# The first batch of an mLSTM and FNet kernel, moved to half chunks

## The chip, the cores and the metric

The kernel runs on one core of a Trainium2 chip. Its time is the device time of one execution in microseconds (us); several executions are timed and the median is given. The core has five instruction streams that run beside each other and wait for one another through semaphores: PE (TensorE, matrix products, with its weight loads), DVE (VectorE), ACT (ScalarE), POOL (GpSimd), and SP (SyncE, which here only issues transfers between memories). Each stream works strictly in the order written into it.

## The reference, cut to what matters

Two blocks are chained. The first is a gated recurrence over 768 tokens, for 4 batches of 8 heads with 40 features each:

```python
for t in range(S):
    m_new = np.maximum(f_gate[:, :, t] + m, i_gate[:, :, t])
    f_stab = np.exp(f_gate[:, :, t] + m - m_new)
    i_stab = np.exp(i_gate[:, :, t] - m_new)
    m = m_new
    C = f_stab[..., None, None] * C + i_stab[..., None, None] * np.einsum('bhd,bhe->bhde', vt, kt)
    n = f_stab[..., None] * n + i_stab[..., None] * kt
    h_tilde = np.einsum('bhde,bhe->bhd', C, qt)
    denom = np.maximum(np.abs(np.einsum('bhd,bhd->bh', n, qt)[..., None]), 1.0)
    y[:, :, t] = sigmoid(o_gate[:, :, t]) * h_tilde / denom
```

The second takes the heads side by side as 320 features per token and does

```python
u = x + real(fft(fft(x, axis=1), axis=2))       # over tokens, then over features
un = (u - mean(u)) / sqrt(var(u) + 1e-6)        # per token
out = u + relu(un @ w_ch1) @ w_ch2              # 320 -> 1280 -> 320
```

The two weight matrices arrive as 64-bit floats and are turned into 32-bit ones on the chip, piece by piece.

## The kernel before, in words

Tokens are worked on in 6 chunks of 128 per batch. The recurrence becomes, in each chunk, scores of keys against queries weighted by exponentials of running maxima, plus the queries times the state of all earlier chunks. The 768x768 transform uses symmetries: chunks are paired as (0,5), (1,4), (2,3), and three of them (`BACKWARDS` = 0, 1, 3) hold their tokens in reverse order, so that sums and differences of a pair ("folds", `mix_fold`) go straight into the products (`mix_seq`, `mix_tail`). Then come the products over features (`mix_feat`), the sum with x and its mean and variance (`mix_add`), centring and transposing (`mix_center`, `mix_turn`, `mix_turn_out`), and the two layers (`mlp_in` and so on).

The order of all work is written out by hand: `at(slot, phase, function, arguments)` puts a step into a plan, and the plan is emitted in order of slot and phase, into each engine's list. The slots run over the whole kernel: the recurrence of batch 0 lies in slots 0 to 21, its transform in 16 to 30, its layers from slot 31; the recurrence of batch 1 lies beside the layers of batch 0, and so on. Before the plan, `gates()` computes cumulative sums and running maxima of the gates for all batches at once, on 32 rows (batch and head) by 768 tokens.

Batches 1 to 3 use the *half-chunk form* (`plan_halves`, functions `halves_...`): chunks are split in two halves of 64 tokens; maxima and decays are read back from DRAM copies (`M_d`, `G_d`) spread over rows; results come out with tokens on partitions; for a backward chunk, `halves_rows` moves the result to its place in x by two or three transfers. The products of one chunk are issued in the order: queries times state, half of the within-chunk products, scores of the next chunk, new state of the next chunk, the other half.

Batch 0 uses the *whole-chunk form* (`plan_mlstm`, functions `mlstm_...`): maxima are spread over 128 rows by products with a unit column (`spread_max`, L221), weights have 128 keys by 128 queries per head (`mlstm_exp` L491, `mlstm_weigh` L545), results come out with features on partitions (`mlstm_from_state` L553, `mlstm_from_chunk` L560), are copied by ACT (`mlstm_gather`, L583 to L601), transposed by PE (`mlstm_turn`, L611), and finished by DVE (`mlstm_finish`, L712 to L720) directly into x. What batches 1 to 3 need in half-chunk form is made late from batch 0's arrays (`halves_of_chunks`, L329 to L362; `other_halves`; `maxima_out`).

SP's list holds all transfers: inputs `qk` (two transfers a chunk), `kvt`, `so`; the pieces of the weights (`raw`, 0.66 MB each, loaded by `Piece.load`, then `take` on DVE, `convert` on ACT, `join` on DVE); the tables of the transform (`load_tables`: `ds_sb` 1.18 MB, `dd_sb` 0.66 MB); `Gb` (decays spread from `G_d`). Eight completion semaphores are used in turn, so a transfer is issued only when the one eight places earlier has landed.

Of the kernel before, what the change touches and what calls it, by code (L numbers as in the profile page):

```python
# [10 lines left out]
FP = mybir.dt.float32  # L11
BF = mybir.dt.bfloat16
# [3 lines left out]
OP = mybir.AluOpType  # L16
# [37 lines left out]
def kernel(  # L54
# [28 lines left out]
    ps_early = ExitStack()  # L83
    ps_s, ps_h = (ps_early.enter_context(tc.tile_pool(name=n, bufs=2, space=PSUM)) for n in ("ps_s", "ps_h"))

    turn = iter("3210321032120312031230123012012301023130201320132013203120123021320321")
# [17 lines left out]
    h_first = const.tile([L, NP, 1], FP, name="h_first")  # L104
# [6 lines left out]
    C_bufs = [const.tile([L, NP, L], FP, name=f"C{n}") for n in range(3)]  # L111
    states = [t.rearrange("p n t -> p (n t)")[:, i * 2 * L:(i + 1) * 2 * L] for t in C_bufs for i in range(2)]
# [3 lines left out]
    Cd_bufs = [s_last[:, n * NP * D1:(n + 1) * NP * D1].rearrange("p (n m) -> p n m", m=D1) for n in range(2)]  # L116
    hT_bufs = [const.tile([L, NP, L], FP, name=f"h{n}") for n in range(2)]
# [18 lines left out]
    def idle_products(n, first=False):  # L136
        pw = bank("pi", [L, 2 * L]) if first else ps_s.tile([L, 2 * L], FP, name="pi", tag="ps")
        for i in range(n):
            nc.tensor.matmul(pw, rest[:, 0:L], rest, start=True, stop=True, skip_group_check=True)


    def gates(gp):
        f_sb = gp.tile([BH, NT, L], FP, name="f_sb")
        free = w2_sb.rearrange("p f m -> p (f m)")
        M, a = (free[0:n, (i + 1) * S:(i + 2) * S].rearrange("p (c t) -> p c t", t=L) for i, n in enumerate((L, BH)))
        nc.sync.dma_start(out=f_sb.rearrange("p c t -> p (c t)"), in_=f_gate.rearrange("b h s -> (b h) s"))
        nc.sync.dma_start(out=a.rearrange("p c t -> p (c t)"), in_=i_gate.rearrange("b h s -> (b h) s"))
        keep = gp.tile([BH, NT, L], FP, name="keep")
        shift = gp.tile([BH, NT, L], FP, name="shift")
        m_in = gp.tile([BH, NT, 1], FP, name="m_in")  # L150
        F = gp.tile([BH, NT, L], FP, name="F")
        g, wk = (x_bufs[1].rearrange("p c m -> p (c m)")[0:n, i * S:(i + 1) * S].rearrange("p (c t) -> p c t", t=L)
                 for i, n in enumerate((L, BH)))
        nM = gp.tile([BH, NT], FP, name="nM")
        M3 = gp.tile([3 * BH, NT, L], BF, name="M3")
        below = gp.tile([BH, NT, L], BF, name="below")
        sel = gp.tile([3 * BH, BH], BF, name="sel")
        ident_b, later_b = (gp.tile([L, L], BF, name=n) for n in ("ident_b", "later_b"))
# [7 lines left out]
        nc.gpsimd.memset(later_b, 0.0)  # L166
        nc.gpsimd.affine_select(out=later_b, in_=later_b, compare_op=OP.is_ge, fill=-M_INIT, base=0, pattern=[[1, L]],
                                channel_multiplier=-1)
        nc.scalar.copy(out=ident_b, in_=ident)
        for i in range(3):  # L170
            nc.scalar.copy(out=sel[i * BH:(i + 1) * BH], in_=ident[0:BH, 0:BH])
# [3 lines left out]
        nc.vector.memset(M[:, 0:2], 0.0)  # L175
        for t in C_bufs:
            nc.scalar.copy(out=t.rearrange("p (two n) t -> p two (n t)", two=2),
                           in_=rest.unsqueeze(1).to_broadcast([L, 2, 2 * L]))
# [7 lines left out]
        w1_pieces[1].load()  # L186
        for t in hT_bufs + Cd_bufs + [h_first]:
            nc.gpsimd.memset(t, 0.0)

        def flat(t, s):  # L190
            return t[0:BH, s].rearrange("p c t -> p (c t)")
# [5 lines left out]
        def maxima(s, initial):  # L197
            c0, c1 = s.start, s.stop
# [5 lines left out]
            nc.vector.tensor_scalar(out=nM[:, s], in0=M[0:BH, s, L - 1], scalar1=-1.0, scalar2=None, op0=OP.mult)  # L204
# [1287 lines left out]
```

## Time and profile before

| | us |
|---|---|
| median of 3 executions | 391.76 (391.52 to 393.21) |
| the profiled execution, its own time | 392.19 |
| span of its instructions | 390.4 |
| PE busy in the span | 379.6 (97%) |
| DVE busy | 278.0 (71%) |
| ACT busy | 172.1 (44%) |
| POOL busy | 134.9 (35%) |
| mean granted clock of PE | 0.999 |

The profiled execution's own time is 1.8 us more than its span and 0.4 us above the median. A line of a timeline reads: start, length, engine, line of the kernel, operation, output<-input, shape, count; in brackets the idle time before it and what ended it. A line of the stage table reads: stretch, its length, busy time of PE, PEld (weight loads), DVE, ACT and POOL with counts of instructions, PE's granted clock, the share of the 16 DMA engines that was busy, and GB/s.

### The profile page before, as it was taken

How to read it: one execution, taken by the hardware profiler on the slowest of the kernel's cores; microseconds unless marked ns; L12 is line 12 of the kernel's file. 1: busy time of each engine (PE TensorE's matmuls, PEld its weight loads, DVE VectorE, ACT ScalarE, POOL GpSimd, SP SyncE). 2: the span in 40 equal slices, each digit the busy share in tenths (PEclk: the TensorE clock that was granted, in tenths of full speed). 3: DMA queues.
4: the chain of work that ended last, by engine and by line, in shares of the span. 5: the costliest groups of instructions: out<-in, count | busy, mean ns of one | idle time of the engine just before them, and what ended most of it. 6: DMA issues, size and time to landing. Idle time of an engine off the chain costs nothing.

```text
span 390.4 us, 10585 instructions
## 1 busy us (share of the span) xinstructions
PE 379.6 (97%) x4174; PEld 277.3 (71%) x4174; DVE 278.0 (71%) x671; ACT 172.1 (44%) x481; POOL 134.9 (35%) x237
## 2 busy tenths in 40 slices
PE   8999899999999999999999999999999999999996
PEld 6777555656667777765569998755588996556996
DVE  7789988499599587476975699777655785346652
ACT  6887357477543233655462314554530133545000
POOL 5739504467954442173254134541500000020000
PEclk9999999999999999999999999999999999999999
DMA  7887499579394345437700626400000000000101
GB/s 224 287 235 204 159 254 255 179 214 271 109 231 116 122 116 150 149 102 184 182 2 28 174 80 192 135 20 2 0 2 34 6 30 34 2 0 0 35 34 35
DMA packets 25631, 44.78 MB, mean 115 GB/s; under 512 B 5727, under 2 KB 14766, under 8 KB 25454
## 3 DMA queue, kind: packets, MB, share of 16 engines
q1 hardware_dynamic: 25582, 44.11, 38.9%
q8 instruction: 33, 0.54, 0.6%
q14 instruction: 16, 0.13, 0.1%
HBM read 38.49 MB, written 4.12 MB: 109 GB/s over the span
## 4 chain that ended last, share of the span: by engine, by line
PE 78%; DVE 14%; issue 3%; ACT 3%; POOL 1%; DVEq 0%; ACTq 0%; POOLq 0%
PE po L1240 20%; PE pm L1121 15%; PE po L1184 8%; PE pm L1059 7%; PE ph L519 4%; PE pm L1126 4%; PE pu L938 4%; PE ps L519 3%; PE pm L1050 2%; PE put L981 2%; PE pz L907 1%; PE pz L895 1%; DVE h L1130 1%; DVE so L716 1%; PE pM L221 1%
## 5 line engine op out<-in xcount | busy, mean ns | idle before, releaser
L1190 DVE SCALAR_TENSOR_TENSOR x<-po,rstd,x 128x160 f32<-128x160 f32 (+1 forms) x69 | 27.1, 394 | 37.4 <-PE po L1240 32.5
L1130 DVE TENSOR_TENSOR h<-h,pm 128x384 f32<-128x384 f32 x60 | 30.5, 548 | 27.1 <-PE pm L1121 12.6
L652 POOL TENSOR_TENSOR C<-C,decB 128x164 f32<-128x164 f32 x30 | 15.9, 531 | 67.5 <-DVE C L667 56.1
L1121 PE MATMUL pm<-uT,w_sb 128*128 128x384 f32 x90 | 37.7, 506 | 1.3 <-DVE uT L1109 0.6
L491 ACT ACTIVATE W<-W,colT 128x64 f32<-128x64 f32 x144 | 37.5, 339 | 0.4 <-DMA W<-M_d 0.4
L1184 PE MATMUL po<-w_sb,h 128*128 128x320 f32 x120 | 34.3, 435 | 0.0
L515 POOL TENSOR_SCALAR_AFFINE_SELECT W<-W 64x512 f32<-64x512 f32 x36 | 27.3, 759 | 10.6 <-ACT W L491 9.1
L1005 POOL TENSOR_TENSOR t<-rstd 128x6 f32<-128x6 f32 x12 | 3.3, 273 | 79.9 <-DVE v L999 79.4
L1059 PE MATMUL pm<-uT,w_sb 128*128 128x384 f32 x80 | 29.2, 500 | 0.1
L1184 PEld LDWEIGHTS po<-w_sb,h 128*128 128x128 f32 x120 | 22.3, 190 | 9.5 <-issue 0.6
L1240 PE MATMUL po<-T,S 128*128 128x160 f32 x180 | 27.8, 301 | 0.3 <-DVE x L1190 0.3
L501 POOL TENSOR_TENSOR qg<-qk,Gb 128x512 f32<-128x512 f32 (+1 forms) x21 | 27.1, 1290 | 1.7 <-DMA qk<-in_qkT 1.6
L1240 PEld LDWEIGHTS po<-T,S 128*128 128x128 f32 x180 | 25.5, 190 | 1.7 <-DVE x L1190 0.5
L1121 PEld LDWEIGHTS pm<-uT,w_sb 128*128 128x128 f32 x90 | 15.5, 189 | 15.6 <-DVE h L1130 6.7
L1240 PE MATMUL po<-w_sb,h 128*128 128x160 f32 x180 | 26.3, 300 | 0.0
L1240 PEld LDWEIGHTS po<-w_sb,h 128*128 128x128 f32 x180 | 25.2, 190 | 1.4 <-DVE x L1190 0.3
L986 ACT COPY uT<-put 128x384 f32<-128x384 f32 x24 | 11.2, 477 | 30.1 <-PE put L981 30.1
L507 POOL TENSOR_TENSOR vw<-kvt,colT 128x328 f32<-128x328 f32 x23 | 19.7, 859 | 13.1 <-DMA qk<-in_qkT 10.1
L1177 ACT ACTIVATE h<-h 128x384 f32<-128x384 f32 x45 | 23.1, 520 | 2.0 <-DVE h L1130 2.0
L1126 PE MATMUL pm<-uT,w1t_sb 64*128 64x384 f32 x120 | 23.4, 508 | 0.0
L1059 PEld LDWEIGHTS pm<-uT,w_sb 128*128 128x128 f32 x80 | 14.1, 189 | 9.6 <-issue 1.9
L974 ACT ACTIVATE uc<-x 128x384 f32<-128x384 f32 x24 | 14.4, 613 | 12.6 <-DVE x L966 11.1
(241 smaller groups left out, 843.4 us busy)
## 6 DMA issues: line engine op xcount, KB each, us to landing
kvt<-in_kv SPq DMA_DIRECT2D x24, 336.0 KB
qk<-in_qkT SPq DMA_DIRECT2D x48, 160.0 KB
raw<-in_w SPq DMA_DIRECT2D x10, 640.0 KB
Gb<-G_d SPq DMA_DIRECT2D x36, 128.0 KB
W<-M_d SPq DMA_DIRECT2D x36, 128.0 KB
so<-in_o SPq DMA_DIRECT2D x24, 160.0 KB
out<-x SPq DMA_DIRECT2D x24, 160.0 KB
x<-so SPq DMA_DIRECT2D x9, 140.0 KB
```

Source lines behind the costliest of these rows:

```text
L491: nc.scalar.activation(out=k.W[:, h, :], in_=M, func=AF.Exp, scale=-1.0, bias=colT[:, c, 0, b * H + h:b * H + h + 1])
L501: nc.gpsimd.tensor_tensor(out=k.qg[:, :, t], in0=k.qk[:, 0, :, t], in1=k.Gb[:, :, t], op=OP.mult)
L515: nc.gpsimd.affine_select(out=W, in_=W, compare_op=OP.is_ge, fill=0.0, base=base, pattern=[[0, H], [step, LH]], channel_multiplier=-1)
L519: nc.tensor.matmul(out, w, x, start=start, stop=True, skip_group_check=True)
L1059: nc.tensor.matmul(k.pm[i], w1_sb[:, ch, f0:f0 + L], u[2 * ch], start=(ch == 0 and not ahead), stop=(ch == 1 and ahead), skip_group_check= ...
L1121: nc.tensor.matmul(bank, w, u, start=start, stop=True, skip_group_check=True)
L1126: nc.tensor.matmul(bank, block(w1t_sb, i)[rows], mlp_u(gr, 1)[rows], start=False, stop=True, skip_group_check=True)
L1130: nc.vector.tensor_tensor(out=h, in0=h, in1=bank, op=OP.add)
L1177: nc.scalar.activation(out=h, in_=h, func=AF.Relu, scale=-1.0)
L1184: nc.tensor.matmul(k.po[gr, i], hidden(gr, f)[:, i * L:(i + 1) * L], w2_sb[:, f, :], start=(f == 0), stop=(f == NFF - 1))
L1190: nc.vector.scalar_tensor_tensor(out=u, in0=po, scalar=k.rstd[:, c:c + 1], in1=u, op0=OP.mult, op1=OP.add)
L1240: nc.tensor.matmul(po, a[:, f], w[:, f], start=start and f == 0, stop=f == half - 1, skip_group_check=True)
```

## The change

Batch 0 takes the half-chunk form as well; `plan_mlstm` and its functions go, and `plan_first` orders the halves functions for batch 0. Its parts:

- `gates()` works out maxima, decays and key weights for halves from the start, for all batches; `halves_of_chunks` and `other_halves` go. The keys' terms are the biases of the exponentials. The maxima of a chunk are spread by 16 products over 64 columns instead of 8 over 128, into one bank instead of two. Key weights of chunks 2 to 5 are exponentiated in one ACT instruction (`weights_of_others`), and so prepared by one DVE instruction; the same is done for the decays (`decays_of_others`).
- Results come out with tokens on partitions: no transposes, no whole-chunk copies; ACT copies one chunk's result out of the accumulators (`halves_heads`) and DVE finishes from that copy. Chunks 0, 1 and 3 of batch 0 get to x by transfers (`halves_rows`), and chunk 2 passes one row over POOL and one transfer.
- The decays go to DRAM in three transfers early (`decay_out`) and the maxima at slot 6 instead of 12 (`maxima_out`).
- The weights' second piece is loaded at slot 7 instead of ahead of the plan; the pieces' conversion steps are placed later, with three buffers for raw pieces instead of two.

The diff, cut to its core:

```diff
+        def decay_out(c0, c1, h0, t=slice(0, L)):
+            nc.sync.dma_start(out=G_d[c0:c1, h0:, t].rearrange("c p t -> p c t"), in_=gq[h0:, c0:c1, t])
...
+        def weights_of_others():
+            nc.vector.tensor_tensor(out=halves(wk)[:, 2:], in0=halves(a)[:, 2:], in1=over_halves(nM), op=OP.add)
+            nc.scalar.activation(out=wk[:, 2:], in_=wk[:, 2:], func=AF.Exp)
+
+        def decays_of_others():
+            nc.vector.tensor_tensor(out=halves(F)[:, 2:], in0=over_halves(m_in), in1=halves(m)[:, 2:], op=OP.subtract)
+
+        def spread_max(c):
+            k = chunks[0, c]
+            k.M = bank("pM", [L, H, LH])
+            nc.tensor.matmul(k.M, ident_b, later[:, int(c in BACKWARDS)].unsqueeze(1).to_broadcast([L, H, LH]), start=True,
+                             stop=False, skip_group_check=True)
+            w, x = (ident[:, 0:H], m_all) if c < 2 else (sel, M3)
+            for h in range(H):
+                for j in range(2):
+                    nc.tensor.matmul(k.M[rows(j), h], w[:, h:h + 1].to_broadcast([w.shape[0], LH]),
+                                     x[:, c, rows(j ^ (h & 1))], start=False, stop=True, skip_group_check=True)
...
-        at(12, FILL + 0.7, maxima_out)
-        at(13, FILL + 0.7, other_halves)
...
+                (1, FILL, decay, (2,)), (3, FILL + 0.15, parts, (3, 4)), (3, FILL_PE + 4, spread_decay, (1,)),
+                (3, FILL_PE + 5, columns, (2, NT, 1)), (4, FILL + 0.3, columns_out, (2, NT, 1)), (1, FILL + 0.1, decay, (3,)),
+                (1, FILL + 0.4, decay_out, (1, 4, 0)), (5, FILL + 0.15, parts, (4, 6)), (5, FILL + 0.4, decay, (4,)),
+                (5, FILL + 0.5, decay, (5,)), (5, FILL + 0.6, decay_out, (4, 6, 0)),
+                (5, FILL + 0.65, decay_out, (0, 1, H, slice(0, LH))), (6, FILL_PE + 4, spread_decay, (2,)),
+                (6, FILL + 0.9, maxima_out, ()),
...
+    def halves_heads(b, c):
+        k = chunks[b, c]
+        h = tp.tile([L, 2, NP, D1], FP, name="heads", tag="heads")
+        nc.scalar.copy(out=h, in_=k.ph)
+        k.ph = h
...
-        k.x = k.so if b > 0 and c in BACKWARDS else xs[b][:, c, 0:DM]
+        k.x = k.so if c in BACKWARDS else xs[b][:, c, 0:DM]
...
+    def plan_first():
         for c in range(NT):
-            s = s0 + stride * c
+            s = 3 * c
+            if c > 1:
+                at(s - 2, FILL, mlstm_exp, 0, c, 0)
+                at(s - 2, FILL, mlstm_exp, 0, c, NP)
+                at(s - 1, FILL, mlstm_scale_v, 0, c)
             if c > 0:
+                at(s + 2 if c < 3 else s, FILL + 0.1, mlstm_scale_q, 0, c)
+                at(s, FILL_PE + 2.05, halves_scores, 0, c)
+                at(s, FILL_PE + 2.5, halves_to_state, 0, c)
+                at(s + 1, FILL - 0.3, halves_weigh, 0, c)
+                for i in range(2):
+                    at(s + i, FILL + 0.05, halves_decay, 0, c, i)
+                    at(s + 1 + i, FILL - 0.2, halves_add, 0, c, i)
             end = c == NT - 1
+            t = s + 2 if end else s + 3
+            at(t, FILL_PE, halves_from_state, 0, c)
+            at(t, FILL_PE, halves_from_chunk, 0, c, 0)
+            at(t, FILL_PE + 0.5, halves_between, 0, c)
+            at(t, FILL_PE + 0.6, mlstm_tanh, 0, c)
+            at(*((19, FILL_PE) if end else (t, FILL_PE + 3)), halves_from_chunk, 0, c, 1)
+            at(20 if end else t + 1, FILL - 0.5, halves_heads, 0, c)
+            at(*((21, FILL + 0.05) if end else (17 if c == 4 else t + 1, FILL + 0.3)), mlstm_finish, 0, c)
+            if c < 4:
+                at(s + 5, FILL - 0.6, halves_rows, 0, c)
...
-    when = [((2, 0.7), (4, 0.5), (6, 0.6)), ((6, 0.7), (7, 0.5), (8, 0.6)), ((11, 0.7), (13, 0.5), (22, 0.6))]
-    when += [((22, 0.7), (23, 0.7), (31, 0.5)), ((31, 0.7), (32, 0.7), (33, 0.6))]
+    when = [((5, 0.7), (6, 2.65), (8, 0.6)), ((17, 0.7), (18, 0.7), (22, 0.6)), ((22, 0.7), (23, 0.7), (31, 0.5))]
+    when += [((31, 0.7), (32, 0.3), (33, 0.6)), ((33, 0.65), (34, 0.1), (35, -0.1))]
...
-    early = [(3, mlstm_load, 3), (3, mlstm_load_o, 2), (4, mlstm_load, 4), (5, mlstm_load_decay, 3),
-             (5, mlstm_load_decay, 4), (6, None, 2), (7, mlstm_load_o, 3), (7, mlstm_load, 5),
-             (11, mlstm_load_decay, 5), (11, None, 3), (11, mlstm_load_o, 4), (12, load_tables, None),
-             (14, mlstm_load_o, 5), (23, None, 4)]
+    early = [(3, mlstm_load, 3), (3, mlstm_load_o, 2), (3, mlstm_load_decay, 3), (5, mlstm_load, 4), (6, mlstm_load_o, 3),
+             (7, mlstm_load_decay, 4), (7, None, 1), (8, mlstm_load, 5), (9, mlstm_load_decay, 5), (9, mlstm_load_o, 4),
+             (10, None, 2), (12, load_tables, None), (12, mlstm_load_o, 5), (13, None, 3), (23, None, 4)]
```

`halves_rows` (unchanged, now called for batch 0 too) moves a backward chunk's result from `so` to x:

```python
        if c == 2:
            nc.gpsimd.tensor_copy(out=x[0:1, 1], in_=x[0:1, 2])
            nc.gpsimd.tensor_copy(out=x[0:1, 2], in_=x[0:1, 0])
            move(x[0:1, 0], chunks[b, 1].x[L - 1:L])
        elif c in BACKWARDS:
            n = L - L // 8
            move(x[1:n + 1, c], y[0:n])
            move(x[n + 1:L, c], y[n:L - 1])
            if c != 1:
                move(x[0:1, c], y[L - 1:L])
```

## The prediction, made before the changed kernel was run

> **What bounds the kernel now.** I read the page first (PE 97% busy), then the chain of waits up to the layers, then each engine's timeline and SP's, then a table of stages. From 59.54 us on, where the layers of batch 0 begin, PE is busy almost without a gap and the change leaves its work there as it is. So what counts is when that first layer product starts. Ahead of it, in the chain:
>
> ```profile
> 46.22 0.87 POOL eo L827
> ...
> 48.02 0.91 PE pz L907 x2
> 48.93 0.80 PE pzt L907 x4
> 49.73 1.49 PE pz L907 x4
> 51.22 0.80 PE pzt L907 x4
> 52.02 1.83 PE pu L938 x6
> ...
> 53.88 0.50 DVE x L958
> ...
> 59.01 0.49 ACT uT L986
> ...
> 59.54 0.59 PE pm L1059
> ```
>
> DVE's timeline has the folds that feed these products; the first begins at 41.30 and the last ends at 49.89 (8.6 us, in DVE's order with the finishes of chunks 4 and 5):
>
> ```profile
> 41.30 0.74 DVE L815 TENSOR_TENSOR eo<-x 128x320 f32<-128x320 f32 x1
> ...
> 49.57 0.32 DVE L822 TENSOR_TENSOR fe<-eo 128x159 f32<-128x159 f32 x1
> ```
>
> SP's timeline and the stage table show the transfers behind that:
>
> ```profile
> 2.88 0.43 SPq L484 DMA_DIRECT2D so<-in_o  x1
> ...
> 7.19 0.35 SPq L456 DMA_DIRECT2D kvt<-in_kv  x1
> ...
> 16.10 0.31 SPq L291 DMA_DIRECT2D G_d<-x  x1
> ...
> 35.83 0.58 SPq L438 DMA_DIRECT2D ds_sb<-in_dft_s  x1
> 36.46 0.43 SPq L439 DMA_DIRECT2D dd_sb<-in_dft_d  x1
> 37.00 0.36 SPq L484 DMA_DIRECT2D so<-in_o  x1
> ```
>
> ```profile
> 8.00:16.00 8.00, 7.95 (x108) 6.88 (x109) 6.45 (x12) 6.10 (x22) 5.43 (x7) 1.00 0.98 358
> 16.00:25.00 9.00, 8.18 (x117) 6.56 (x112) 7.04 (x13) 7.96 (x24) 3.51 (x9) 1.00 0.67 192
> 25.00:34.00 9.00, 8.60 (x134) 7.25 (x132) 8.51 (x13) 6.66 (x23) 6.42 (x12) 1.00 0.93 270
> 34.00:37.00 3.00, 2.75 (x33) 2.19 (x32) 2.83 (x10) 2.74 (x7) 2.65 (x6) 1.00 0.23 56
> 37.00:43.00 6.00, 5.18 (x72) 4.60 (x74) 5.59 (x17) 3.82 (x13) 3.99 (x7) 1.00 0.92 332
> ```
>
> The transfers nearly fill three stretches; the tables, issued at 35.83 to 36.89, flow until 42.6. Bytes moved to 43 us (248 GB/s mean, 10.7 MB) equal the sum of what was issued (10.6 MB). They also come in order: the kvt issue at 7.19 waits for the so issued at 2.88; by then 1.27 MB had moved, and all issued through that so is 1.03 MB. The next three such waits give 1.44 against 1.20, 1.69 against 1.36, 2.03 against 1.70. Each landing is its place in the list plus about 1 us of flow.
>
> **The engines in the changed kernel.** *Start.* DVE clears 128x384 more (0.38, scaled from the 0.27 of 128x256), so it scans first at 3.50 instead of 3.12. Its list then holds, each by its row of before: scan, difference, maximum scan and row copies of chunk 0 (to 5.05); the same for the others (1.47 + 0.80 + 1.54 and six small ones, to 10.4); then, waiting on PE between them, weigh 0.68, state copy 0.33, qg 0.35, dec 0.45, decB 0.35, the joint key weights 0.65, an add 0.31, the joint decays 0.65. It ends near 15.5. The joint exponential (32x512, some 0.55) replaces four of the five that took 1.55 and saves ACT about 0.7, but ACT waits for DVE here, so nothing of it is on the path. ACT's decays of chunks 2 and 3 (0.4 + 0.6) follow, and the decay transfer is issued at 16.5, against 16.10 before.
>
> *Per chunk.* PE falls from about 5.3 (products 1.09 + 1.09 + 1.00 + 0.60, maxima 0.9, transposes 0.6) to about 2.9 (0.84 + 0.81 + 0.36 by the rows of batch 1, maxima 0.9; sixteen narrow products in place of eight may make these 0.7 to 1.1, and I keep the row). ACT: eight exponentials of 64 columns took 2.02 in batch 1 against 2.18 of 128 columns here, so nothing is won; with the warm copy 0.13, tanh 0.47 and heads copy 0.48 it has 3.1, against 3.9 before. DVE has 0.68 + 2x0.31 + 1.55 = 2.9. The loop runs over two chunks (exponentials 2.02, weigh 0.68, add 0.31, state products 0.5, chunk products 0.24, next scores and states 0.9, second products 0.36, heads 0.48, hand-overs 0.5): 6.0, so about 3.1 a chunk, in place of some 5.6. Chunks 1 and 2 carry more: DVE qg 0.68, PE pG 1.02 and the first weight piece (take 1.0, convert 1.5, join 2.45), about 6 each. On POOL, chunk 2's two row copies (0.44 each) wait for chunk 2's finish, and chunk 4's vw (0.74) and qg (1.28) are queued behind them: 2 more for PE. From the second products of chunk 0 at 16.9 that gives 22.2 for chunk 1, 28.4 for chunk 2, 33.9 for chunk 3; with heads 0.48 and finish 1.6 chunk 3 is done at 36.0. Bounds: 34.4 (POOL's wait hidden) and 37.5 (a join lengthened beside POOL, as one part of it was to 1.84 at 25.32).
>
> **The new wait.** Before, DVE wrote x itself and the first fold waited for no transfer. Now it needs chunk 3 in x by three transfers (0.56 an issue in the median of the later ones), issued at about 36 to 38. Fold, finish of chunk 4, a weight piece's take, second fold and finish of chunk 5 stand behind it in DVE's list; ACT's convert, queued on that take, holds the last heads copy. In SP's list tables, an so and a weight piece are ahead of these transfers. Ahead of the decay transfer SP has issued only 3.2 MB, moved by 12.5, where before the queue stayed full to 16 (4.3 MB): 4 us of flow are lost. The next 2.3 MB keep pace with SP (issues 0.35 to 0.75 each, Gb 1.25 a pair, M_d 3.6 for four, moved ahead of chunk 4's Gb from slot 12) until 28.7. From there to chunk 3's landing: two Gb pairs, and 5.13 MB (weight pieces 1.97, tables 1.84, qk and kvt 0.67, so 0.33, x 0.33). A Gb pair costs 1.9 us of flow: between 20 and 34 the queues were busy 11.9 us, of which 2.3 MB of large transfers take 6.2 at 0.37 MB/us, and three pairs the rest. Large ones run at 0.36 (37 to 43) to 0.40 (38 to 42) MB/us: 12.8 to 14.2. Sum 28.7 + 3.8 + 12.8 to 14.2 + 0.5 = 45.8 to 47.2. With no idle flow at all after 17.5 (7.94 MB, 25.6 us) it is 43.6. If order did not count, issue end 38.4 plus 1.9 (f_sb issued 0.80 to 1.20, scanned at 3.12) gives 40.3. I take 46.0, since the four landings above follow the order.
>
> [...]
>
> **Behind the fold.** Fold start to last fold 8.8 instead of 8.6. From there the former path lost 0.65 to the second fold's POOL work (46.22, behind L342 and L347, which go), and 0.45 to L354, L355 and the DVE copies L358 to L362 (1.0): 0.2 - 0.65 - 0.45 = -0.9. After the layers start, one more weight piece (3.45 DVE, 1.55 ACT) falls into DVE idle of 2.21 and 2.64 at 68 to 75; ACT's convert stands ahead of two relus whose bank PE wants 12.5 after the start, and I find them done at 12.3: 0 to 0.8, taken 0.3. By the above PE idles some 6 us before the first product on a fold. Its first products show the price of a cold start: 0.49 a pass of L139 against 0.22 at 57.2. On the path lie 1.49+0.80+1.83 = 4.1, so 0 to 4.1; products run from 7 us earlier on and nearest rows from 6.7 are full speed, so 0.7.
>
> [...]
>
> Sum: (46.0 - 41.3) - 0.9 + 0.3 + 0.7 = +4.8 on 392.19, the profiled execution's own time, so 397.0. That execution is 0.43 above the median: 396.6.
>
> **Rivals.**
> 1. Transfers overtake: fold at 40.3, no cold start: -1.0 - 0.9 + 0.3 = -1.6: 390.2. For it: nothing in the trace lands late enough to forbid it. Against: the four waits.
> 2. Faster: SP reaches the tables early enough that they have landed when chunk 3 is written (36.0 + 0.35 + 1.9 = 38.2): -3.1 - 0.9 + 0.3 = -3.7: 388.1. It decides where the fold starts before 39.9; tables and piece need 7 us of flow, so they must be issued before 31. For it: M_d issues could be short (0.60 at best). Against: a transfer ahead of the tables waits for chunk 2's finish, near 31.5.
> 3. PE cold through the tail: 4.1 instead of 0.7: 400.0. For it the slow first passes, against it that products precede.
>
> **How the numbers follow.** Chances: forecast 0.55 (fold at 44 to 48: 393.8 to 399.3), rival 1 0.12, rival 2 0.20, rival 3 0.13. Half a per cent, 2.0 us, is about what can be told from no change: slower 0.55 + 0.13 = 0.68, same 0.12, faster 0.20. The range 388.4 to 401 holds forecast, rivals 1 and 3 and half of rival 2.
>
> **What would show it.** Right: DVE idle for 5 us or more before the first fold, released by an x<-so transfer; flow below 0.5 between 12 and 16; PE idle beside it; heads of chunk 4 long done. Wrong: a first fold near 38 to 40; flow that ends before it; first layer product before 59.

## The result and the profile after

The changed kernel takes 409.33 us (median of 409.20 to 412.13), the kernel before beside it 391.64: a ratio of 1.046 [1.041, 1.051], slower by 17.7 us. The forecast had the direction right and the wait that it put at the centre; its size was wrong: 396.6 was said, and 409.3 lies outside its range. The step that failed lies ahead of that wait: the recurrence, whose products it took at PE's full clock (2.9 to a chunk, where rows at half clock add to 5.6), and which ends 8.8 later than said. A ratio leaves out executions more than 1.5% above the fastest of their kernel; all_eased, eased_md_early and eased_raw_early have one each, which their medians below include. The profiled execution's own time is 409.31, its span 407.3.

| start in us | before | forecast | after |
|---|---|---|---|
| decay transfer | 16.10 | 16.5 | 18.89 |
| second products of chunks 0, 1, 2, 3 | | 16.9, 22.2, 28.4, 33.9 | 19.16, 25.21, 34.87, 41.27 |
| chunk 3 finished (end) | 40.19 | 36.0 | 44.79 |
| tables issued | 35.83 | | 41.79 |
| first fold | 41.30 | 46.0 | 55.57 |
| last fold (end) | 49.89 | 54.8 | 65.96 |
| first layer product | 59.54 | | 75.05 |
| from there to the end of the span | 330.9 | | 332.3 |

The fold is 14.27 later, fold to last fold takes 1.80 more, last fold to layers 0.56 less, the rest 1.39 more: 16.9, the difference of the spans.

The chain of waits answers to the one shown of before. Columns: start, length, what was waited for.

```profile
40.68 5.71 DMA raw<-in_w
...
46.41 9.03 DMA x<-so
...
55.57 0.50 DVE eo L724
```

SP's timeline (an engine name with a q is its issuing) and DVE's, where the first fold stands:

```profile
18.89 0.34 SPq L302 DMA_DIRECT2D G_d<-x  x1
...
41.79 0.58 SPq L422 DMA_DIRECT2D ds_sb<-in_dft_s  x1
42.42 0.43 SPq L423 DMA_DIRECT2D dd_sb<-in_dft_d  x1
43.36 0.33 SPq L466 DMA_DIRECT2D so<-in_o  x1
44.00 0.33 SPq L380 DMA_DIRECT2D raw<-in_w  x1
44.85 2.08 SPq L630 DMA_DIRECT2D x<-so  x3
```

```profile
28.12 0.33 DVE L562 TENSOR_TENSOR C<-C,ps 128x164 f32<-128x164 f32 x1 [1.90 <-POOL C L547]
...
50.21 0.32 DVE L562 TENSOR_TENSOR C<-C,ps 128x164 f32<-128x164 f32 x1
55.57 0.49 DVE L724 TENSOR_TENSOR eo<-x 128x320 f32<-128x320 f32 x1 [5.04 <-DMA x<-so]
```

This is the wait that was forecast: DVE stands 5.04 before its first fold, and x<-so, issued from 44.85, lands near 55.5, behind tables, so and raw piece. Only everything ahead of it is late: the tables are issued 6 later than before, and chunk 3 is finished 8.8 later than forecast. PE's timeline and its table of stretches (length, busy time of PE, weight loads, DVE, ACT, POOL; granted clock, DMA share, GB/s) say why:

```profile
9.92 1.98 PE L245 MATMUL pM<-w_sb,ident 128*64 128x64 f32 x32 [1.72 <-DVE w_sb L212]
...
24.26 0.70 PE L504 MATMUL ps<-qk 40*64 40x64 f32 x32
...
31.83 1.26 PE L504 MATMUL ph<-C,qg 40*64 40x41 f32 x30 [4.61 <-DVE qg L485]
...
38.26 1.13 PE L504 MATMUL ps<-qk 40*64 40x64 f32 x32
...
41.26 0.22 PE L504 MATMUL ps<-vw,kvt 64*40 64x41 f32 x1 [0.76 <-issue]
...
49.14 0.29 PE L504 MATMUL ps<-vw,kvt 64*40 64x41 f32 x2 [2.67 <-issue]
```

```profile
8.00:10.00 2.00, 0.28 (x3) 0.08 (x4) 1.97 (x7) 1.09 (x5) 1.99 (x4) 0.76 1.04 354
14.00:18.00 4.00, 2.87 (x50) 2.18 (x52) 2.49 (x7) 1.32 (x5) 1.28 (x3) 0.50 0.01 4
...
32.00:38.00 6.00, 6.00 (x193) 5.38 (x192) 5.77 (x11) 2.17 (x10) 1.32 (x2) 0.50 0.62 156
38.00:45.00 7.00, 5.34 (x153) 4.12 (x149) 3.47 (x9) 3.15 (x16) 4.71 (x7) 0.50 0.98 271
45.00:50.00 5.00, 2.18 (x64) 1.88 (x64) 0.41 (x2) 0.47 (x2) 1.69 (x2) 0.50 1.01 410
50.00:58.00 8.00, 2.54 (x50) 1.94 (x50) 2.83 (x9) 0.91 (x3) 2.26 (x5) 0.50 0.83 246
58.00:62.00 4.00, 3.67 (x25) 2.34 (x26) 3.93 (x7) 2.00 (x3) 2.91 (x5) 0.50 0.00 1
62.00:66.00 4.00, 4.00 (x15) 1.57 (x11) 3.70 (x12) 0.00 (x0) 0.67 (x1) 0.79 0.00 0
```

Three things are new against the kernel before, whose clock read 1.00 in each of the stages shown. PE's clock is 0.50 in most of the recurrence, and the same 32 score products take 1.13 where they took 0.70 at 24.26. PE idles 4.61 ahead of chunk 2's state products, since DVE's qg comes late (the add of DVE at 28.12 waits 1.90 for a state decay that stands behind the split of the maxima of chunks 4 and 5 in POOL's list, and DVE's finish of chunk 1 stands between that add and qg). And PE has waits of 0.76 and 2.67 named issue: the profile shows nothing that the engine waited for.

### The profile page after: what moved, and what is told of

The parts are those of the page before. It is cut to its first block, busy times and chain, and to the rows that moved or that the text cites. A ratio compares the mean times of both kernels' runs of the same rounds, so it can differ in the third digit from the quotient of the medians.

```text
span 407.3 us, 11495 instructions
## 1 busy us (share of the span) xinstructions
PE 379.7 (93%) x4624; PEld 275.8 (68%) x4624; DVE 280.1 (69%) x680; ACT 165.6 (41%) x480; POOL 135.2 (33%) x239
## 4 chain that ended last, share of the span: by engine, by line
PE 67%; DVE 15%; DMA 9%; issue 3%; POOL 2%; ACT 2%; SPq 1%; DVEq 0%; POOLq 0%
PE po L1149 19%; PE pm L1030 14%; PE po L1093 8%; PE pm L968 4%; PE pm L1035 4%; PE ph L504 4%; PE ps L504 3%; DMA qk<-in_qkT 3%; PE pu L847 2%; DMA raw<-in_w 2%; DMA x<-so 2%; DMA kvt<-in_kv 2%; PE pz L804 1%; DVE so L618 1%; PE put L890 1%
## 5 line engine op out<-in xcount | busy, mean ns | idle before, releaser
L547 POOL TENSOR_TENSOR C<-C,decB 128x164 f32<-128x164 f32 x40 | 21.8, 546 | 74.8 <-DVE C L562 53.8
L478 ACT ACTIVATE W<-W,colT 128x64 f32<-128x64 f32 x144 | 37.5, 339 | 0.0
L504 PE MATMUL ph<-kvt,W 64*64 64x41 f32 x768 | 24.7, 244 | 2.0 <-issue 1.2
L1030 PEld LDWEIGHTS pm<-uT,w_sb 128*128 128x128 f32 x90 | 15.5, 189 | 15.6 <-DVE h L1039 6.7
L504 PEld LDWEIGHTS ph<-C,qg 40*64 40x64 f32 x704 | 15.7, 151 | 14.8 <-issue 11.2
L567 DVE TENSOR_TENSOR W<-ps,W 128x512 f32<-128x512 f32 x24 | 16.4, 685 | 13.3 <-PE ps L504 10.6
L492 POOL TENSOR_TENSOR vw<-kvt,colT 128x328 f32<-128x328 f32 x24 | 21.3, 889 | 8.1 <-ACT colT L278 6.6
L504 PE MATMUL ph<-C,qg 40*64 40x41 f32 x704 | 18.6, 245 | 5.7 <-DVE qg L485 5.1
```

Of the source, the lines that this page charges most:

```text
L478: nc.scalar.activation(out=k.W[:, h, :], in_=x[:, h, :], func=AF.Exp, scale=-1.0, bias=colT[:, c, 0, b * H + h:b * H + h + 1])
L492: nc.gpsimd.tensor_tensor(out=k.vw, in0=k.v1, in1=colT[:, c, 1, b * H:(b + 1) * H].unsqueeze(2).to_broadcast([L, H, D1]), op=OP.mult)
L504: nc.tensor.matmul(out, w, x, start=start, stop=True, skip_group_check=True)
L547: nc.gpsimd.tensor_tensor(out=halves_state(k, i + 1), in0=halves_state(k, i), in1=decB[:, b * NP:(b + 1) * NP, n].unsqueeze(2).to_broadcas ...
L1030: nc.tensor.matmul(bank, w, u, start=start, stop=True, skip_group_check=True)
```

## The experiments

Median, ratio to the kernel before, and from the profile of each: end of chunk 3's finish, start of the first fold, first layer product. The last column is the time of that one execution.

| run | median | ratio | finish | fold | layers | this |
|---|---|---|---|---|---|---|
| the changed kernel | 409.33 | 1.046 [1.041, 1.051] | 44.79 | 55.57 | 75.05 | 409.31 |
| tables_after | 408.35 | 1.040 [1.035, 1.046] | 46.19 | 49.57 | 72.24 | 409.46 |
| x_other_queue | 411.52 | 1.050 [1.047, 1.053] | 44.81 | 49.57 | 76.43 | 409.96 |
| tables_first | 402.99 | 1.030 [1.023, 1.038] | 45.42 | 50.14 | 69.09 | 401.58 |
| tables_first_raw_late | 403.29 | 1.031 [1.028, 1.035] | 46.20 | 49.59 | 68.73 | 403.53 |
| parts_later | 410.40 | 1.048 [1.044, 1.052] | 42.91 | 57.07 | 76.59 | 410.05 |
| warm_pe | 411.25 | 1.051 [1.047, 1.056] | 53.18 | 59.14 | 81.75 | 414.48 |
| warm_gaps | 407.31 | 1.040 [1.034, 1.045] | 41.80 | 52.80 | 72.25 | 404.94 |
| gates_split | 409.93 | 1.046 [1.043, 1.049] | 44.12 | 54.94 | 74.39 | 409.56 |
| tables_first_parts | 405.75 | 1.034 [1.029, 1.039] | 42.75 | 50.76 | 70.67 | 405.40 |
| three_causes | 405.33 | 1.033 [1.030, 1.037] | 44.08 | 50.74 | 70.17 | 405.34 |
| before_x_moved | 396.92 | 1.013 [1.012, 1.015] | 39.08 | 44.48 | 63.74 | 396.64 |
| all_eased | 397.01 | 1.011 [1.007, 1.016] | 40.84 | 44.13 | 63.01 | 395.91 |
| eased_no_idle | 403.21 | 1.029 [1.028, 1.031] | 44.37 | 47.66 | 66.80 | 403.99 |
| eased_md_early | 399.07 | 1.016 [1.011, 1.020] | 39.45 | 45.73 | 65.71 | 398.73 |
| eased_raw_early | 401.60 | 1.021 [1.014, 1.028] | 38.46 | 45.19 | 64.72 | 397.08 |

### The new wait alone, in the kernel before

```diff
-        k.x = k.so if b > 0 and c in BACKWARDS else xs[b][:, c, 0:DM]
+        k.x = k.so if (b > 0 and c in BACKWARDS) or (b, c) == (0, 3) else xs[b][:, c, 0:DM]
...
+        if (b, c) == (0, 3):
+            for r in (slice(0, L - L // 8), slice(L - L // 8, L - 1), slice(L - 1, L)):
+                move(x[r, c], y[r])
...
+            if c == 3:
+                at(x, FILL + 0.06, halves_rows, b, c)
```

> One part of the change alone, in the kernel before: chunk 3's result is written by DVE into its so buffer, and three x<-so transfers of 112, 15 and 1 rows bring it to x, issued behind the tables (37.4) when the finish of chunk 3 is done (40.1). Everything else is as before (fold 41.30, layers 59.54). Order theory: issues at 40.1 to 42, the tables flow until 42.6, the transfers land at 43.5 to 45, fold 2.2 to 3.7 later, layers 2 to 3.5 later: 394 to 395.5. So in the old recurrence the new wait costs some 3, and the rest of the 14.3 by which the fold moved is the recurrence, its transfers and PE's clock. If the transfers cost as much as in the changed kernel by themselves (10.7 from issue to landing): fold at 50, time 400.

```profile
38.59 0.49 DVE L720 TENSOR_TENSOR so<-px,so 128x320 f32<-128x320 f32 x1
39.00 1.28 DVE L545 TENSOR_TENSOR W<-ps,W 128x512 f32<-128x512 f32 x2
44.48 0.49 DVE L820 TENSOR_TENSOR eo<-x 128x320 f32<-128x320 f32 x1 [4.21 <-DMA x<-so]
```

```profile
44.00:46.00 2.00, 0.11 (x1) 0.11 (x1) 1.45 (x5) 0.45 (x2) 1.40 (x2) 0.78 0.00 0
46.00:48.00 2.00, 1.38 (x4) 0.87 (x5) 1.72 (x5) 0.00 (x0) 1.88 (x6) 0.50 0.00 0
```

DVE's timeline and PE's stretches: the fold is 3.2 later, as expected, and PE, idle meanwhile, runs its transform products at 0.50: last fold to layers takes 10.9 (63.74 - 52.80) instead of 9.65. Together 4.2 at the layers and 5.0 in the time [4.5, 6.0 by the interval of the ratio]. That is more than I expected of this run, and it is near what the forecast had put on the whole change, +4.8. The agreement is in part luck: the fold moved by 3.2 where 4.7 was said, and the cold products cost 1.3 where 0.7 was said. What the forecast had not seen is the other 12.7.

### The order of the transfers

```diff
 # tables_after
-             (10, None, 2), (12, load_tables, None), (12, mlstm_load_o, 5), (13, None, 3), (23, None, 4)]
+             (10, None, 2), (14, load_tables, None), (14, mlstm_load_o, 5), (15, None, 3), (23, None, 4)]
 # tables_first
-        mlstm_load(0, 2)
+        mlstm_load(0, 2); load_tables()
-             (10, None, 2), (12, load_tables, None), (12, mlstm_load_o, 5), (13, None, 3), (23, None, 4)]
+             (10, None, 2), (12, mlstm_load_o, 5), (13, None, 3), (23, None, 4)]
 # tables_first_raw_late: also
-             (10, None, 2), (12, mlstm_load_o, 5), (13, None, 3), (23, None, 4)]
+             (12, mlstm_load_o, 5), (14, None, 2), (15, None, 3), (23, None, 4)]
 # x_other_queue
-            nc.sync.dma_start(out=out, in_=in_)
+            (nc.scalar if (b, c) == (0, 3) else nc.sync).dma_start(out=out, in_=in_)
```

> The tables, the last so and the third raw piece are issued after the three x<-so transfers of chunk 3 instead of before them; nothing else is moved. Changed kernel: chunk 3 finished at 44.8, x<-so issued 44.85 to 46.93, fold at 55.57, first layer product at 75.05, time 409.3. Order theory (the fold waits for the bytes that stand ahead in one list): without 2.6 MB ahead (1.84 tables, 0.16 so, 0.66 raw) the fold starts near 49 (issue end 46.9 plus about 2). The tables are then issued at 46.9 and land near 53, so products start at 53 instead of 57, the last fold ends near 60 (fold plus 10.4), layers near 69 to 71: 403 to 405. Clock theory (what is late is the recurrence, and a fold after 10 us is what such a transfer needs): fold still at 54 to 56, time 409 or above. If SP's list is what holds the whole stretch back, the tables come 2 later than they could and the gain is under 2.

> The two tables (1.84 MB) are issued at 7.4, behind the second kvt, where SP has nothing to do until the decay transfer at 18.9 and the flow is near zero from 14 to 18, instead of at 41.8; nothing else is moved. Order theory: x<-so of chunk 3 then has 1.84 MB less ahead of it, 4.8 us at 0.38 MB/us, so that the fold starts at 48 to 51 (55.57 in the changed kernel; issue end plus 1.3 is the floor, as in the run with the tables behind), and the products no longer wait for ds_sb: last fold near 60, layers at 68 to 70, time 402 to 405. Rival: the tables only shift the delay into the recurrence, because kvt and qk of chunks 1 and 2 or the so behind them come late; then chunk 1 is finished later than 30.85 and the time stays at 408 or above. [...]

> As the run with the tables first, and the raw pieces 2 and 3 (0.66 MB each) are issued behind the x<-so transfers of chunk 3 instead of ahead of them. Order theory: nothing large is left ahead, the fold starts 1.3 to 2 after the end of the issues, at 46 to 48; layers at 66 to 68, time 400 to 403. Rival: from here the recurrence sets the end (chunk 3 finished at 44.8), and the fold gains nothing over the run with the tables first alone; or the raw pieces come late for their conversion (slots 17 to 31) and the layers wait for weights: then the time is the same or higher than there.

> The three x<-so transfers of chunk 3 are issued by ACT, behind its last exponential (end 44.84), instead of by SP; the tables and the rest stay where they are. Order theory: the transfers stand in another list than the tables and share the 16 DMA engines with them, so they land 2 to 4 us after their issue (44.9 to 46.9): fold at 48 to 51. The tables (issued 41.8 to 42.9) land near 53, so products start near 53, last fold ends near 60, layers near 69 to 70: 403 to 405. If the engines serve the bytes in order of arrival whatever the queue, fold at 54 to 56 as in the changed kernel (55.57) and time 408 to 410.

With the tables behind, the fold starts at 49.57, 3.4 after chunk 3 is finished (10.8 in the changed kernel): the order theory holds for the fold. The time did not follow. The products now wait for ds_sb, as PE's timeline of tables_after has it:

```profile
55.14 0.98 PE L813 MATMUL pz<-ds_sb,fe 128*128 128x193 f32 x2 [4.52 <-DMA ds_sb<-in_dft_s]
...
97.51 0.19 PE L504 MATMUL ph<-kvt,W 64*64 64x41 f32 x1 [1.91 <-issue]
```

In the profiled execution the layers start 2.8 earlier, and 2.9 are given back behind that: a wait of 1.91 at 97.51, and the clock at 0.91 in the 20 us around it. With the tables first, 6.3 are won (the intervals of the two ratios do not touch): the fold starts 4.7 after the finish and waits for no transfer any more. It stands behind a weigh of chunk 5 that waits for PE, as DVE's timeline of tables_first has it:

```profile
49.30 0.69 DVE L567 TENSOR_TENSOR W<-ps,W 128x512 f32<-128x512 f32 x1 [3.64 <-PE ps L504]
49.91 0.32 DVE L562 TENSOR_TENSOR C<-C,ps 128x164 f32<-128x164 f32 x1
50.14 0.48 DVE L724 TENSOR_TENSOR eo<-x 128x320 f32<-128x320 f32 x1
```

So 6 of the 10.8 between finish and fold are the price of the tables' place, and moving two issues to where SP stood idle gives them back. Moving the raw pieces as well gave nothing in that version: the fold stands 3.4 behind the finish, so what is left ahead of it is mostly the recurrence.

The run on ACT's queue is inconclusive. Its first fold is early (49.57), but SP stood from 37.0 to 47.34 ahead of chunk 5's Gb, and tables, so and raw pieces came 10 late. ACT issued the moved transfers only from 44.90, and in the chain of waits an x<-so that ends at 49.35 stands directly ahead of the second issue of that Gb (49.36): SP's list waited for the moved transfers. That shared completion semaphores tie the two lists together is the author's reading; no run shows it.

### What holds the recurrence back

```diff
 # parts_later
-                (1, FILL + 0.4, decay_out, (1, 4, 0)), (5, FILL + 0.15, parts, (4, 6)), (5, FILL + 0.4, decay, (4,)),
+                (1, FILL + 0.4, decay_out, (1, 4, 0)), (7, FILL + 0.1, parts, (4, 6)), (5, FILL + 0.4, decay, (4,)),
 # warm_gaps
-        spread_max(1)
+        idle_products(4, 2); spread_max(1)
...
+    for s, phase, n, f in ((9, -0.1, 10, 2), (24, 5.5, 1, 0), (25, 5.5, 1, 0), (26, 5.5, 1, 0)):
 # warm_pe: the same with
+        (6, 4.1, 8, 2), (9, 4.1, 2, 2), (12, 4.1, 2, 2), (15, 4.1, 3, 2), (17, 4.1, 8, 2)
 # gates_split
-            nc.scalar.activation(out=wk[:, 2:], in_=wk[:, 2:], func=AF.Exp)
+            for c in range(2, NT):
+                weights(c)
```

(`idle_products(n, 2)` writes n products of zeros to unused columns of the heads' bank.)

> The five POOL copies and differences that split the maxima of chunks 4 and 5 (24.77 to 27.5 in the changed kernel) move behind the two state decays of chunk 2 that stood after them. List theory: the decay at 27.62 runs at 24.8, so DVE's add (28.12) follows the weigh at 26.2, the finish of chunk 1 and qg of chunk 2 (31.00) come 2 to 2.8 earlier, PE's idle of 4.61 ahead of 31.83 shrinks to about 2, chunk 3 is finished near 42.3 instead of 44.8, and the time falls by 2 to 2.8: 406.5 to 407.5. Rival, SP's list: SP issues without pause from 18.89 to 44.33 and reaches the x<-so transfers of chunk 3 no earlier than 44.3, so the fold moves by 0.5 at most and the time by less than 1. Clock theory: with the gap down to 2 the clock stays at 1.00 after 30 and chunk 3 is finished near 40.

> PE is given idle products of 128x256 on zeros where it waits: 4 ahead of the maxima of chunk 1 (idle of 1.72 ahead of 9.92), 8 ahead of the state products of chunk 2 (idle of 4.61 ahead of 31.83), 2 ahead of those of chunks 3 and 4, 3 ahead of those of chunk 5, and 8 ahead of the first fold's products. Clock theory: the granted clock stays at 1.00 or nearly from 8 to 64 (0.50 in 10 to 22 and 30 to 62 in the changed kernel); PE's part of a chunk falls from 4.9 to 3.3, the decay transfer from 18.89 to about 17.5, chunk 3 is finished near 40 and the fold starts 3 to 5 earlier: 404 to 406. Rival: the clock rises, but SP's list and the queue set the fold all the same, so that the time falls by 1.4 at most (the earlier decay transfer).

> Idle products of 128x256 in two places where PE only waits and where no other engine waits for them: 4 ahead of the maxima of chunk 1 and 10 directly ahead of the state products of chunk 2. Clock theory: in the run with idle products in six places the first four alone kept the clock at 1.00 until about 15 and brought the decay transfer forward by 1.5 or more; the same here (17.2 instead of 18.89). The ten then fill 27.2 to about 31, PE restarts warm, and the granted clock stays near 1.00 afterwards; PE's part of a chunk falls from 4.9 to 3.3, chunk 3 is finished at 41 to 42 instead of 44.8. What that is worth: 3 to 4 us (405 to 406) if the recurrence sets the fold; at most 1.8 (the earlier start, as SP's whole list moves) if SP's list and the queue do. Rival: the small half-chunk products do not hold the clock, and it is back at 0.50 a few us after 32 though PE is busy.

> One part of the change is undone: key weights and decays of chunks 2 to 5 are exponentiated per half chunk by ACT with biases (8 and 8 instructions of 0.29) instead of being prepared by two DVE instructions (0.67 each) and exponentiated in joint ones. ACT is free from 14.7, so the weights end near 17.0 and the decays of chunks 2 and 3 near 18.1: the decay transfer at 18.1 instead of 18.89, and all of SP's list 0.8 earlier. If the joint form costs on the path: time lower by 0.5 to 1. If it costs nothing (as forecast): within 0.5 of the changed kernel.

parts_later brings PE's idle time from 4.61 to 2.77 and chunk 3's finish forward by 1.9, but x<-so keeps its place behind the tables (SP reaches it at 45.88) and the fold is 1.5 later: an earlier recurrence alone is worth nothing here. The rival of that run (SP's list sets the fold) was right. gates_split brings the decay transfer forward by 1.3 and the time not at all: the joint exponentials cost nothing, as forecast.

warm_pe was badly placed. ACT's copies of the heads had to wait for idle products written to the same tile (7.15, 5.13 and 5.53 ahead of three of them), so chunk 3 was finished at 53.18, and its products in slot 17 stand between the two halves of chunk 5's accumulation: this version returns other values than the rest (relative error 0.106). Only its start is of use: the decay transfer at 17.09. warm_gaps repeats that start and fills the one long gap:

```profile
9.95 1.15 PE L245 MATMUL pM<-w_sb,ident 128*64 128x64 f32 x32
...
31.49 0.68 PE L504 MATMUL ph<-C,qg 40*64 40x41 f32 x32
...
36.41 0.69 PE L504 MATMUL ps<-qk 40*64 40x64 f32 x32 [1.18 <-DVE C L562]
...
42.09 1.45 PE L504 MATMUL ps<-qk 40*64 40x64 f32 x29 [1.03 <-DVE C L562]
```

The 32 maxima products of chunk 1 take 1.15 instead of 1.98, the decay transfer comes 1.8 earlier, chunk 3 is finished 3.0 earlier, and the profiled fold 2.8. Of the time 2.0 are won, by intervals that overlap a little. The clock does not last: after waits of 1.17 and 0.88 it is lost at 15.90 (the 32 score products take 1.13 there, 0.69 at 6.45) until about 25, and after waits of 1.18 and 0.78 ahead of small products it is lost again near 39 (the 32 state products take 1.10 at 39.53).

> The tables issued first and the split of the maxima moved behind the state decays of chunk 2, without idle products. The split alone brought chunk 3 forward, but the fold not (57.07): x<-so was issued at 45.9, at its place behind the tables. With the tables gone the earlier recurrence should count: fold 2 to 3 earlier than with the tables first alone (50.14), at 47 to 48, time 400 to 401 (402.99 there). The difference to the run with three edits is then the price of the clock: 2 to 4 by the clock theory, 0 if PE's pace is not what holds the recurrence back.

> Three edits of earlier runs together: the tables issued first, idle products on PE in two places (4 ahead of the maxima of chunk 1, 4 ahead of the state products of chunk 2), and the split of the maxima of chunks 4 and 5 behind the state decays of chunk 2. Alone they gave -6.3, -2.0 and +1.1 (medians, changed kernel 409.33). If the order of transfers and the late recurrence are two prices that add once the transfers no longer hide the recurrence: chunk 3 finished near 39 to 40 (44.8), x<-so issued from 40.5, fold at 44 to 46, layers at 63 to 65, time 395.5 to 398. If the edits only exchange one wait for another, as the third did alone (fold 57.07 instead of 55.57): 400 to 403, as with the tables first alone.

Neither did what I expected: by the medians they are 2 to 3 slower than the tables first alone (the intervals overlap), though chunk 3 is finished earlier. In three_causes the clock had not come up when the idle products ran: eight records take 3.78, in warm_gaps 1.99, and the decay transfer is at 20.65. So the same idle products cost 1.9 times as much here, where there was no full clock to keep. And x<-so, issued at 44.14 in three_causes and 43.28 in tables_first_parts, lands at 50.7 in both, behind the two raw pieces. The recurrence's lateness had hidden these.

### All together, and one cause put back at a time

all_eased has the three edits, and raw pieces 2 and 3 as well as M_d behind x<-so, and gates_split; the other three each take one edit back.

```diff
 # all_eased, beside tables_first, parts_later, gates_split, raw pieces as above
+        idle_products(4, 2); spread_max(1)
+    for s, phase, n, f in ((9, -0.1, 4, 2), (24, 5.5, 1, 0), (25, 5.5, 1, 0), (26, 5.5, 1, 0)):
-                (6, FILL + 0.9, maxima_out, ()),
+                (14, FILL + 0.9, maxima_out, ()),
```

> The three edits, and further: raw pieces 2 and 3 and the four transfers of M_d behind the x<-so transfers of chunk 3, and the key weights and decays exponentiated by halves. [...] Expected: PE's waits named issue below 1 before the fold, chunk 3 finished at 38 to 39, fold at 42.5 to 44.5, layers at 61.5 to 63.5, time 393.5 to 396. Rival: raw pieces and M_d late take their price in the layers (weights) or in batch 1: no faster than the run with three edits.

> The run with all edits (397.0, single times 394.6 to 404.1) without its idle products on PE. Clock theory: the clock falls near 9 or 14 and again near 28 as in the changed kernel, the recurrence ends 1 to 3 later (chunk 3 finished at 42 to 44 instead of 40.84), time 398 to 400. If what counts is SP's list and the flow alone: within 1 of 397.

> The run with all edits, but the four transfers of M_d go back to slot 6, ahead of chunk 4's Gb. SP's list then holds 2.6 more ahead of x<-so. If SP's list holds the recurrence back (Gb, qk and kvt of chunks 4 and 5 stand behind M_d): chunk 3's finish or its transfers 1.5 to 2.6 later, time 398.5 to 399.6. If not: 397, and these transfers were moved at no gain.

> The run with all edits, but raw pieces 2 and 3 (0.66 MB each) go back ahead of the x<-so transfers of chunk 3. By the order of transfers the flow ahead of x<-so is 1.3 MB longer, 3.5 us at 0.38 MB/us, of which what flows while the recurrence is still at work is hidden: fold 1 to 3.5 later (44.13), and PE's waits named issue come back beside the full flow at 36 to 43 (1 to 2.5 each, 0 with the pieces behind): time 399 to 402. If with the tables first there is room for both, as the earlier pair of runs said (402.99 and 403.29): 397.

397.01 instead of 409.33: 12.3 of the 17.7 are back with every product of the change in place, by the order of transfers and steps, by idle products that hold the clock for a part of the recurrence (0.94 from 8 to 16, 0.89 and 0.96 from 24 to 36, 0.50 from 16 to 24 and from 36 to 44; 0.62, 0.75, 0.53, 0.50 and 0.50 in eased_no_idle), and with the joint exponentials split. It is still 1.1% slower than the kernel before, and its fastest execution (394.64) is slower too; no version here beats the kernel before. Put back, the raw pieces ahead of x<-so cost 4.6 (intervals that overlap by a little) and M_d 2.1 (not told from nothing). Without the idle products the time is 6.2 longer by the medians and 7.1 by the ratios (intervals far apart), more than the clock theory had said. The same rows in PE's timeline of eased_no_idle and then of all_eased:

```profile
9.92 1.98 PE L245 MATMUL pM<-w_sb,ident 128*64 128x64 f32 x32 [1.53 <-DVE w_sb L212]
...
31.98 1.16 PE L504 MATMUL ps<-qk 40*64 40x64 f32 x30
...
91.96 0.90 PE L890 MATMUL put<-ident,uc 128*128 128x128 f32 x3 [1.78 <-issue]
```

```profile
9.95 1.15 PE L245 MATMUL pM<-w_sb,ident 128*64 128x64 f32 x32
...
29.66 0.67 PE L504 MATMUL ps<-qk 40*64 40x64 f32 x32
```

Not all of this is the halved clock in the recurrence. Of the 8.1 between the two profiled executions, 3.8 are there when the layers start (66.80 against 63.01); 4.3 come behind them. There eased_no_idle has the wait of 1.78 at 91.96, named issue, and the eight 128x384 products behind it take 4.01 at 92.66; all_eased has no such wait at these products, and the same eight take 2.75 at 86.70. Taking the idle products out also changes the places of all later products in PE's list. No run puts in as many instructions without keeping the clock, so what the clock alone is worth was not settled beyond the 3.8.

For the raw pieces it is the new wait again, in DVE's timeline of eased_raw_early, where chunk 3 is finished earliest of all (38.46) and x<-so issued from 39.31:

```profile
45.19 0.49 DVE L724 TENSOR_TENSOR eo<-x 128x320 f32<-128x320 f32 x1 [3.46 <-DMA x<-so]
```

## Why the forecast was right about the wait and wrong about the size

**The wait (step "The new wait")**: right. DVE idles 5.04, released by x<-so; the order of the list decides. Rival 1 (transfers overtake) fell: from the issue of x<-so to the fold it took 10.7, and from the end of its issues only 1.3 where the tables stood behind it (tables_after). Rival 2 needed the tables issued before 31, and SP came to them at 41.79. In the kernel before, this part alone costs 5.0.

**The flow's arithmetic** (46.0, bounds 43.6 to 47.2): its rates held (0.41 MB/us from 45 to 50), its starting times did not. It let SP keep pace with its list until 28.7 and then counted bytes alone. In fact SP's list went on to set the pace: from the decay transfer to the tables it took 22.9 (18.89 to 41.79), of which the profile names some 4.4 as waits for engines; for the rest SP issues. An earlier start moves the tables (17.09 and 38.78 in warm_gaps), an earlier recurrence without it does not (18.47 and 42.21 in parts_later). From chunk 3's finish to the fold I had 10.0, and it was 10.8.

**Start** (decay transfer at 16.5): the step that failed first. Its rows were rows of a warm PE. With PE idle for 1.72 ahead of chunk 1's maxima, these took 1.98, the products behind them 1.09, 1.12 and 0.92 instead of 0.68, 0.69 and 0.53; the transfer was at 18.89. With the clock kept it was at 17.09 (warm_gaps): 1.8 of the miss of 2.4 is the clock.

**Per chunk** (second products 5.3, 6.2, 5.5 apart): the step that carries the miss. Measured 6.0, 9.7 and 6.4. PE's part was taken as 2.9, from rows at full clock; its rows in the changed kernel at half clock add to 5.6 (1.09 + 0.65 + 1.13 + 0.78 + 0.67 + 0.61 + 0.64), in warm_gaps at full clock to 3.5. Of chunk 2's 9.7, 4.61 are PE's idle time ahead of its state products. POOL's split of the maxima is some 1.9 of it (2.77 are left in parts_later), the rest mostly DVE's finish of chunk 1: I counted POOL's row copies and not this list. In sum chunk 3 was finished 8.8 later than forecast. Of this the idle products won back 3.0 (warm_gaps) and 3.5 (all_eased against eased_no_idle), the moved split 1.9 (parts_later), each in one profiled execution. Even eased, 38.5 to 40.8 were reached and not 36.0: how that rest divides between a clock that is lost again from 15 to 25 and after 35, and waits for POOL, was not settled.

**Rival 3 (PE cold through the tail)**: PE did run slowly, but at another place. I held 4.1 against products behind the fold, and there it cost nothing visible in the changed kernel: the clock (0.50 from 56 to 62) is back at 1.00 at 64, before the last fold ends. The cold PE was in the recurrence, where I took every row as warm. That PE would idle there was to be had from my own numbers, 2.9 of PE to a chunk and 5.3 to 6.2 from one chunk to the next; even with the longer rows it is busy only 0.73 of 16 to 36 (14.60 of 20), against 0.94 before. I did not ask what clock it would have there: 0.67 in these 20 us, where it was 1.00 before.

**Behind the fold**: fold to last fold took 10.4 instead of 8.8; rows of DVE that run beside the second folds on POOL are stretched (1.05, 0.81 and 0.69 for rows of 0.49, 0.49 and 0.17). From the last fold to the layers it was -0.56, where -0.65 - 0.45 and +0.7 for cold products, -0.4 in all, were said. The further weight piece costs nothing that shows; of the 1.39 lost after the layers begin, 0.82 and 0.43 are waits of PE named issue at 99.24 and 193.93.

**The joint exponentials** at nothing: right (gates_split, 409.93 against 409.33).

Of the 12.3 by which the profiled execution is above the forecast, chunk 3's finish has 8.8, finish to fold 0.8, fold to last fold 1.6 and the part behind the layers' start 1.1. The range failed because its bounds were those of the wait, and the recurrence ahead of it was given 34.4 to 37.5. A chain of small products that wait for one another needed the bound "at half clock", which my own row (0.49 a pass against 0.22) would have priced.

## What to carry to other kernels

Here an edit that took work off an engine took its clock with it (PE busy 0.94 of 16 to 36 at a clock of 1.00 before, 0.73 at 0.67 after): where the forecast leaves PE idle between dependent small products, price these at half clock too (1.13 for the 32 score products, 0.70 at full clock) as one end of the range. The transfer put on the critical path cost its place in the list (10.7 from its issue to the fold), and the list's times were set by its own issuing and by what its earlier entries waited for (22.9 from the decay transfer to the tables, some 4.4 of it waits), so forecast the list as a chain of its own. Before tuning, look for a stretch where the issuing engine stands idle and move there what is needed later anyway: two moved issues were worth 6.3 us here.

## What the runs showed of the hardware

**Being busy alone did not bring the clock back.** In tables_first_parts PE is busy for 9.67 of 10 us at 0.50; columns as in the stretches above.

```profile
18.00:28.00 10.00, 9.67 (x214) 8.20 (x208) 6.65 (x18) 6.83 (x26) 3.87 (x8) 0.50 0.53 161
```

Its products are 40x64 and 64x41 for the most part by number. In the changed kernel the clock came back near 23 (0.50 from 21 to 22, 1.00 from 23 to 24) and near 64 (0.50 from 62 to 63, 1.00 from 64 to 65), after a run of 128-row products each time; that is no rule either, since the same run of products at 20 did not bring it in tables_first_parts (the 32 state products behind it take 1.09 at 22.21 there, 0.68 at 23.57 in the changed kernel).

**The clock column can miss it.** In gates_split the column reads 1.00 from 8 to 16, while chunk 1's 32 maxima products take 1.98 as in the changed kernel (1.15 warm). The duration of one shape is the better witness. The loss at 9 is not certain either: of nine profiles without idle products there, six lose the pace after 1.5 to 1.7 of idle time (1.97 or 1.98 for the 32 products), and tables_first_parts keeps it (1.15) after 1.71. In the other two, gates_split and parts_later, PE had not come up at all: the 32 score products ahead of it take 1.13 at 7.22, against 0.69 in the changed kernel, though the column reads 1.00. That, and the waits below, may be why these versions scatter (394.6 to 404.1 in all_eased) where the kernel before, run beside it, keeps within 0.3%.

**PE waits at fixed places for nothing that the profile shows.** In the recurrence the waits named issue stand at the same few products in the runs with the same list, though not each run has each of them. From chunk 2 on, where two follow one another there are 126 or 127 products between them, each with its weight load, so 252 to 254 instructions (the wait of 1.16 or 1.17 ahead of pd, at 13.62 to 17.22, stands outside this: in four runs 307 products lie between it and the next). The page of the profile counts 36 packets in one of two queues named instruction (q8), for 9,248 products and weight loads: 257 to a packet; in the kernel before, 33 packets for 8,348, so 253. The two counts are close; what PE waits for at these places no run shows. Half chunks reach 126 products in some 4 to 5 us (126 in the 3.8 ahead of the wait at 39.81 in parts_later, 127 in the 5.2 ahead of that at 49.14 here), where the kernel before had 270 products in the 20 us from 16 to 36. At the last state product of chunk 3 the wait was 0.30 in x_other_queue, where the flow ahead of it (the share of the DMA engines that was busy) was 0.38, 0.76 in the changed kernel (0.84), 2.40 to 2.45 in two others (1.02 and 0.88). In the remaining five it was 0.84 (0.63, eased_no_idle), 1.33 (0.84), 1.30 (0.94), 2.48 (0.97) and 1.69 (1.02): longer where the flow is fuller, but not in proportion; up to 3.08 were seen at another product (gates_split, beside a flow of 0.98). No run changed the number of products alone.
